# Reading the moving operands of the feed-forward products from the last column to the first

## The chip, the cores and the metric

The kernel runs on one core of a Trainium2 chip, as one launch. The metric is the device time of that launch in microseconds, on the slowest core, which here is the only one. A time is given as the median of several runs. All durations of single instructions come from one further execution that the hardware profiler recorded.

## What is computed

Windowed attention over 4 batches, 8 heads, 768 positions and 64 numbers per head, with block summaries as additional keys, and then a feed-forward layer over the 3072 tokens of 512 numbers (2048 hidden units). Cut to what matters:

```python
k_sum = k.reshape(B, H, nb, block, D).max(axis=3)      # block = 32, nb = 24
v_sum = v.reshape(B, H, nb, block, D).mean(axis=3)
scores = concat([where(|i - j| < 16, q k^T / 8, -1e9), q k_sum^T / 8 + log(block)])
x = softmax(scores) @ concat([v, v_sum])               # heads side by side: 3072 x 512
h = x @ w_in                                           # 512 -> 2048
g = s * maximum(h, 0)**2 + b
out = g @ w_out                                        # 2048 -> 512
```

Everything is float32, and the result is wanted close to float32.

## The kernel before

**Chunks.** The 3072 tokens are cut into 12 chunks `c` of T = 256 tokens, three to a batch. For each chunk the attention is done in four head pairs `p`, and then the feed-forward layer over 16 slices `f` of 128 hidden units.

**Attention.** `scores` (L280) makes the scores of 64 positions against a window of 96 keys and the 24 block keys. VectorE masks them (L323), ScalarE takes the exponentials (L336), VectorE normalizes (L346), and the weights are turned so that the keys stand on the partitions: for chunks 0 to 2 by TensorE (`transposes`, L379), later by VectorE (L368). `values` (L397) multiplies the turned weights `pT` with the values `vw`: the values are the stationary operand, 64 columns of `pT` the moving one, and the result `pav` in PSUM has 64 rows per head and 256 tokens in its columns. So each sub-block `i` of 64 tokens is written to its own 64 columns of `pav` (L413 to L417). For chunk 0 `values_of_means` (L388) adds the block summaries in matmuls of their own. `attended` and `attended_low` copy `pav` to SBUF as `x`.

**Split operands.** The two products of the feed-forward layer are done with operands in a rounded float32 form (`fp32r`). Each operand is held as a high part, rounded to that form, and a low part, the rest: `xh` and `xl` for x, `wh` and `wl` for the weights (both products' weights of a slice `f` in one tile of 1024 columns, 512 for the first and 512 for the second), `gh` and `gl` for g. A product is the sum of three matmuls: low by high, high by low, high by high.

**First product.** `hidden` (L454), for a chunk and a slice: 12 matmuls at L460, for the three terms and the four parts `kc` of 128 of the 512 inputs. The stationary operand is 128 columns of the weights, the moving operand is `x[:, kc]`, 128 partitions by 256 tokens. Two slices share a PSUM tile `ph`. For the first two slices of chunk 0 the same is done at L441 (`first_products`) as the parts of x come.

**Between.** ScalarE takes relu (L468) and square (L474), GpSimd scales and shifts (L481), and a copy and a subtraction make `gh` (L219 or L221) and `gl` (L492).

**Second product.** `project` (L495): 6 matmuls at L504 for a chunk and a slice, two halves `t` of 128 tokens by three terms. The stationary operand is 128 token columns of g, the moving operand is `w[:, 512:]`, the 512 output weights, accumulated over all 16 slices in two PSUM tiles `po`, which `evict` copies out and stores.

**Order.** The order of the work is written down: for the start of the program in a list (`FIRST_ORDER`), and after that by a plan of steps that places four slices of the first product (48 matmuls), then four of the second (24), and between them the attention of a later chunk. Each engine goes through its own queue in that order. All weights are loaded, scaled, converted and split once in the first 100 us or so and then stay in SBUF. `laid_out` arranges the inputs on the host; the weights travel as 64-bit words and are brought to float32 on the chip.

Of the kernel before, what the change touches and what calls it, by code (L numbers as in the profile page):

```python
# [19 lines left out]
P = 128  # L20
B, H, S, D = 4, 8, 768, 64
DM, DFF = 512, 2048
BLOCK = 32
WINDOW = 16
SUB = 64
WIN = SUB + 2 * WINDOW
NB = S // BLOCK
KR = WIN + NB
NSUB = 4
T = NSUB * SUB  # L30
# [5 lines left out]
NF = DFF // P  # L36
# [3 lines left out]
def win_start(st):  # L40
    return min(max(SUB * st - WINDOW, 0), S - WIN)
# [3 lines left out]
def windowed_attention_then_relu2_ffn(ctx, tc, qk, vwin, kt, vt, kq, vrow, wp, out):  # L45


    nc = tc.nc
# [98 lines left out]
    kraw, ksum, vraw, vhalf, vsum = {}, {}, {}, {}, {}  # L147
# [128 lines left out]
    def together(c):  # L276

        return c >= 2
# [109 lines left out]
    def values_of_means(p):  # L388
        pT, o = pT_of.pop((0, p)), o_of[0, p]
        for i in range(NSUB):  # L390
            for e in range(2):
                nc.tensor.matmul(
                    o[64 * e : 64 * e + 64, i * SUB : (i + 1) * SUB], vsum[0][0:KR, 2 * p + e],
                    pT[:KR, e * T + i * SUB : e * T + (i + 1) * SUB], start=False, stop=(i == NSUB - 1),
                )

    def values(c, p):  # L397
        vw, pT = vw_t.pop((c, p)), pT_of[c, p] if c == 0 else pT_of.pop((c, p))
        if c == 0 and p % 2:
            o_of[c, p] = ps_po.tile([P, DM], F32, name="pav", tag="po")  # L400
        elif c < 2 or p % 2 == 0:
            if c == 2:
                o_of[c, p] = ps_s.tile([P, 2 * T], F32, name="pav", tag="ps")
            elif together(c) and p:
                o_of[c, p] = ps_t.tile([P, 2 * T], F32, name="pav", tag="pt")
            else:
                o_of[c, p] = ps_v.tile([P, 2 * T], F32, name="pav")
            if c > 1:
                o_of[c, p + 1] = o_of[c, p][:, T:]
        o = o_of[c, p]  # L410
        for i in range(NSUB):
            for e in range(2):
                oi, pi = o[64 * e : 64 * e + 64, i * SUB : (i + 1) * SUB], pT[:, e * T + i * SUB : e * T + (i + 1) * SUB]  # L413
                if c == 0:
                    nc.tensor.matmul(oi, vw[0:WIN, e, i, :], pi[0:WIN], start=(i == 0), stop=False)
                else:
                    nc.tensor.matmul(oi, vw[:KR, e, i, :], pi[:KR], start=True, stop=True)  # L417
# [17 lines left out]

    ph_of, gg, po = {}, {}, {}

    def first_products(ph, w, x, low, kc, first, last):
        k = slice(kc * P, (kc + 1) * P)
        for n, (a, b) in enumerate(((w_l[w], x), (w_h[w], low), (w_h[w], x))):  # L440
            nc.tensor.matmul(ph, a[:, k], b[:, kc], start=(first and n == 0), stop=(last and n == 2))  # L441

    def hidden_pair(c, f):
        if f % 2 == 0:
            ph_of[c, f // 2] = ps_h.tile([P, 2 * T], F32, name="ph", tag="ph")
        return ph_of[c, f // 2][:, (f % 2) * T : (f % 2 + 1) * T]

    def hidden_part(f, kc):
        if kc == 0:
            hidden_pair(0, f)  # L450
        ph = ph_of[0, f // 2][:, (f % 2) * T : (f % 2 + 1) * T]
        first_products(ph, f, xt[0], xl[0], kc, kc == 0, kc == NKC - 1)

    def hidden(c, f):  # L454
        ph = hidden_pair(c, f)
        terms = [
            (w[f], x, kc) for w, x in ((w_l, xt[c]), (w_h, xl[c]), (w_h, xt[c])) for kc in range(NKC)
        ]
        for n, (w, x, kc) in enumerate(terms):
            nc.tensor.matmul(  # L460
                ph, w[:, kc * P : (kc + 1) * P], x[:, kc], start=(n == 0), stop=(n == len(terms) - 1)
            )

    def activate(c, q, other=0):
# [30 lines left out]
    def project(c, f):  # L495
        if f == 0:
            for t in range(T // P):
                pool, tag = ((ps_t, "pt"), (ps_v, "pav"))[t] if c == 1 else (ps_po, "po")
                po[c, t] = pool.tile([P, DM], F32, name="po", tag=tag)
        gh, gl = (g[:, (f % 2) * T : (f % 2 + 1) * T] for g in gg[c, f // 2])  # L500
        terms = [(gl, w_h[f]), (gh, w_l[f]), (gh, w_h[f])]
        for t in range(T // P):
            for n, (a, w) in enumerate(terms):
                nc.tensor.matmul(  # L504
                    po[c, t], a[:, t * P : (t + 1) * P], w[:, 512:],
                    start=(f == 0 and n == 0), stop=(f == NF - 1 and n == len(terms) - 1),
                )

# [38 lines left out]
    def of(fn, *more):  # L547
# [5 lines left out]
        "u": load_unit, "x": load_values, "L": load_k,  # L553
        "W": keep_warm, "K": k_max, "k": fill_k, "Z": scores_of_maxima, "S": scores, "M": masked, "E": exps,
        "N": normalize, "T": transposes, "C": turned, "V": values, "U": values_of_means, "R": mean_of_rows,
        "F": mean_done, "t": fill_v, "X": attended, "y": attended_low, 
        "Ai": of(scale_weights, "in"), "Ao": of(scale_weights, "out"), "A": of(scale_weights, "both"),
        "Bi": of(convert_weights, "in"), "Bo": of(convert_weights, "out"), "D": of(convert_weights, "both"),
        "Y": hidden_part, "H": hidden, "J": activate, "G": scaled, "a": upper_rows, "b": lower_rows,
        "P": project, "O": evict, "h": upper_weights, "l": lower_weights,  # L560
    }
    ahead = set()
# [19 lines left out]
    for c in range(2, NC):  # L582
        bi, ci = place(c)
        for p in range(NPAIR):
# [3 lines left out]
            m, e0, e1, n, fv, tr, tu, va, xa = (base + lag for lag in lags)  # L588
# [17 lines left out]
            if turns_on_dve(c):  # L606
                for u in range(8):
                    a, k = divmod(u + 8 * (p % 2), 4)
                    then(base + TURN_AT[2 * p + u // 4], TURN, turned_blocks, c, p // 2, a, k)
            else:  # L610
                then(tr, PE_ATT, transposes, c, p)
                then(tu, CHAIN, turned, c, p)
            then(va, VISIT, values, c, p)
            if p % 2 == 0:
                then(xa, ATT, attended, c, p)
# [4 lines left out]
    for i in range(NF, NC * NF):  # L620
        c, f = divmod(i, NF)

        then(i - i % 4, HID, hidden, c, f)
        if f % 2:
            for stage_of in (activate, scaled, upper_rows, lower_rows):
                then(i, CHAIN, stage_of, c, f // 2)
        then((i + 4) | 3, PROJ, project, c, f)
        if f == NF - 1:
            for t in range(T // P):
                then((i + 4) | 3, EVICT, evict, c, t)  # L630
# [7 lines left out]
def laid_out(q, k, v, moe_w_in, moe_w_out, moe_s, moe_b):  # L638

    import numpy as np  # L640

    def turn(x):
        return x.reshape(B, NPAIR, 2, S, D).transpose(0, 1, 2, 4, 3).reshape(B, NPAIR, P, S)

    qT, kT = turn(q), turn(k)
    kq = np.concatenate([kT[0], qT[0, :, :, :T]], axis=-1)
    qk = np.zeros((NC - 1, NPAIR, P, T + NSUB * KR + 2), np.float32)
    qk[..., -2:] = np.concatenate([moe_s, moe_b])
    vwin = np.zeros((NC, NPAIR, P, 2, NSUB, D), np.float32)
    for c in range(NC):  # L650
        bi, ci = divmod(c, PER_B)
        kw = np.zeros((NPAIR, P, NSUB, KR), np.float32)
        for i in range(NSUB):
            w = win_start(NSUB * ci + i)
            kw[:, :, i, :WIN] = kT[bi, :, :, w : w + WIN]
            vwin[c, :, :WIN, :, i] = v[bi, :, w : w + WIN].reshape(NPAIR, 2, WIN, D).transpose(0, 2, 1, 3)
        if c > 0:
            qk[c - 1, :, :, :-2] = np.concatenate(
                [qT[bi, :, :, ci * T : (ci + 1) * T], kw.reshape(NPAIR, P, NSUB * KR)], axis=-1
            )  # L660
    vt = v.reshape(B, 2, 4, NB, BLOCK, D).transpose(0, 1, 2, 3, 5, 4).reshape(B, 2, 4 * NB, D, BLOCK)
    vrow = v[0].transpose(1, 0, 2).reshape(3, 2, P, H * D).transpose(0, 2, 1, 3)
    w_in = moe_w_in.view(np.int64).reshape(NKC, P, NF, P).transpose(2, 1, 0, 3).reshape(NF, P, 512)
    w_out = moe_w_out.view(np.int64).reshape(NF, P, DM)
    return {"qk": qk, "vwin": vwin, "kt": kT, "vt": vt, "kq": kq, "vrow": vrow, "wp": np.stack([w_in, w_out], axis=1)}


# [23 lines left out]
```

## Time and profile before

| what | value |
|---|---|
| median of 3 runs | 615.12 us (614.93 to 615.46) |
| span of the profiled execution | 614.0 us |
| what lies around the span, against the median | 1.1 us |
| instructions in the span | 13522 |
| matmuls | 5240, of them 3456 in the rounded form (2304 of 256 columns at L460 and L441, 1152 of 512 at L504) |
| granted TensorE clock | 1.000 |
| moved by DMA | 66.41 MB, 108 GB/s on the mean |

The times of runs and the profiled execution are different executions, so the span is compared with the median only through the 1.1 us. A profile's mean duration of a matmul is that of its record, from its start to its result. Records of neighbours overlap. How fast matmuls follow each other is read from start to start, or from the length of a piece of the chain divided by its count.

### The profile page before, as it was taken

Reading aid. Unit: us, or ns where it says so; the run is one execution under the profiler, and the core shown is the slowest. Engines: PE = TensorE matmul, PEld = TensorE weight load, DVE = VectorE, ACT = ScalarE, POOL = GpSimd, SP = SyncE. Lnnn points to the kernel's source line nnn. Section 1 sums busy time; section 2 is a strip of 40 time slices with the busy share of each in tenths; the row PEclk is TensorE's granted clock in tenths of the full one; section 3 lists DMA queues with packets and bytes.
Section 4 is the critical chain, followed back from the end, with each engine's and each line's share of the span. In section 5 each row is a group of like instructions: output and inputs, shape, how many; then the busy total and the mean of one; then the engine's idle time right before and its main releaser. Section 6 shows DMA issues by size and latency. Waiting matters only on the chain.

```text
span 614.0 us, 13522 instructions
## 1 busy us (share of the span) xinstructions
PE 602.5 (98%) x5240; PEld 545.7 (89%) x5240; DVE 418.2 (68%) x1126; ACT 276.3 (45%) x712; POOL 138.8 (23%) x275
## 2 busy tenths in 40 slices
PE   6999999999999999999999999999999999999997
PEld 5788899899889998999999899999998999999896
DVE  6999998789489378668758648847848927832211
ACT  5989998262352262263163254235235236223221
POOL 4321012111411411412131411331141151141110
PEclk9999999999999999999999999999999999999999
DMA  8999723026205016103503112500710500200000
GB/s 336 388 394 366 268 83 112 4 96 177 85 3 184 1 45 233 47 20 104 170 20 113 73 45 61 220 18 20 220 55 1 185 4 16 86 1 1 36 1 35
DMA packets 26993, 66.41 MB, mean 108 GB/s; under 512 B 3824, under 2 KB 3824, under 8 KB 26928
## 3 DMA queue, kind: packets, MB, share of 16 engines
q1 hardware_dynamic: 26928, 65.54, 30.3%
q8 instruction: 41, 0.67, 0.4%
q14 instruction: 24, 0.20, 0.1%
HBM read 59.09 MB, written 6.29 MB: 106 GB/s over the span
## 4 chain that ended last, share of the span: by engine, by line
PE 88%; DVE 4%; ACT 3%; DMA 3%; issue 1%; SPq 1%; POOL 0%; POOLq 0%; ACTq 0%; DVEq 0%
PE po L504 40%; PE ph L460 39%; PE pav L417 3%; PE ps L301 3%; ACT pr L336 2%; DVE pT L368 2%; DMA wraw<-in_wp_dram 1%; DMA vsum<-vmean 1%; PE warm L199 1%; DVE pr L346 1%; DMA kq<-in_kq_dram 1%; PE pt L379 1%; SPq L180 0%; POOL vw L263 0%; DVE gl L492 0%
## 5 line engine op out<-in xcount | busy, mean ns | idle before, releaser
L481 POOL TENSOR_SCALAR r<-r,sb_col 128x512 f32<-128x512 f32 x85 | 69.6, 819 | 389.9 <-ACT r L474 247.0
L504 PE MATMUL po<-wh,gl 128*128 128x512 f32 x384 | 150.9, 393 | 0.0
L504 PE MATMUL po<-wl,gh 128*128 128x512 f32 x384 | 149.6, 390 | 0.0
L504 PE MATMUL po<-wh,gh 128*128 128x512 f32 x384 | 149.5, 389 | 0.0
L468 ACT ACTIVATE r<-ph 128x512 f32<-128x512 f32 x93 | 55.3, 595 | 204.9 <-PE ph L460 192.5
L219 DVE CAST gh<-r 128x512 fp32r<-128x512 f32 x88 | 37.7, 429 | 139.5 <-POOL r L481 135.9
L368 DVE STREAM_TRANSPOSE pT<-pr 32x256 f32<-32x256 f32 x288 | 125.5, 436 | 4.1
L460 PE MATMUL ph<-xh,wl 128*128 128x256 f32 x760 | 120.9, 281 | 0.6 <-ACT r L468 0.6
L460 PE MATMUL ph<-xl,wh 128*128 128x256 f32 x760 | 120.2, 281 | 0.0
L460 PE MATMUL ph<-xh,wh 128*128 128x256 f32 x760 | 120.2, 281 | 0.0
L460 PEld LDWEIGHTS ph<-xh,wl 128*128 128x128 f32 x760 | 106.2, 189 | 5.6 <-ACT r L468 1.2
L460 PEld LDWEIGHTS ph<-xh,wh 128*128 128x128 f32 x760 | 103.3, 190 | 0.0
L460 PEld LDWEIGHTS ph<-xl,wh 128*128 128x128 f32 x760 | 102.6, 189 | 0.0
L504 PEld LDWEIGHTS po<-wh,gh 128*128 128x128 f32 x384 | 72.0, 188 | 15.1
L504 PEld LDWEIGHTS po<-wh,gl 128*128 128x128 f32 x384 | 72.1, 188 | 14.5 <-issue 1.0
L504 PEld LDWEIGHTS po<-wl,gh 128*128 128x128 f32 x384 | 72.1, 188 | 12.8
L336 ACT ACTIVATE pr<-pr,mn 128x120 f32<-128x120 f32 x176 | 66.9, 382 | 22.8 <-DVE mn L323 22.7
L492 DVE TENSOR_TENSOR gl<-r,gh 128x512 fp32r<-128x512 f32 x96 | 69.2, 721 | 3.7 <-ACT gh L221 0.9
L474 ACT ACTIVATE r<-r 128x512 f32<-128x512 f32 x92 | 58.1, 632 | 5.3 <-DVE r L470 2.4
L263 POOL COPY vw<-vsum 24x256 f32<-24x256 f32 x88 | 46.8, 564 | 36.9 <-DMA vsum<-vmean 21.8
L346 DVE TENSOR_TENSOR pr<-pr,rs 128x480 f32<-128x480 f32 x48 | 32.5, 678 | 2.4 <-ACT pr L336 0.5
L221 ACT COPY o<-po 128x512 f32<-128x512 f32 x23 | 13.5, 587 | 45.2 <-PE po L504 44.2
(88 smaller groups left out, 479.3 us busy)
## 6 DMA issues: line engine op xcount, KB each, us to landing
wraw<-in_wp_dram SPq DMA_DIRECT2D x32, 512.0 KB
qk<-in_qk_dram SPq DMA_DIRECT2D x44, 369.0 KB
vw<-in_vwin_dram SPq DMA_DIRECT2D x48, 256.0 KB
out_dram<-o SPq DMA_DIRECT2D x24, 256.0 KB
kraw<-in_kt_dram SPq DMA_DIRECT2D x12, 384.0 KB
vraw<-in_vt_dram SPq DMA_DIRECT2D x12, 252.0 KB
kq<-in_kq_dram SPq DMA_DIRECT2D x4, 512.0 KB
vraw<-in_vt_dram SPq DMA_DIRECT2D x6, 264.0 KB
```

The source lines that it names most:

```text
L219: nc.vector.tensor_copy(out_, in_)
L263: nc.gpsimd.tensor_copy(vw_t[c, p][WIN:KR, e], vsum[bi][WIN : WIN + NB, 2 * p + e, :].unsqueeze(1).to_broadcast([NB, NSUB, D]),)
L301: nc.tensor.matmul(o, qi, kw[r, i, :], start=True, stop=True)
L336: nc.scalar.activation(pr, pr, AF.Exp, bias=mn_of[c, p][:, n : n + 1], scale=-1.0, accum_out=sm_of[c, p][:, n : n + 1])
L346: nc.vector.tensor_tensor(pr, pr, rs.unsqueeze(2).to_broadcast([P, 4, KR]), ALU.mult)
L368: nc.vector.transpose(to[BLOCK * k : BLOCK * (k + 1), :, rows], src)
L460: nc.tensor.matmul(ph, w[:, kc * P : (kc + 1) * P], x[:, kc], start=(n == 0), stop=(n == len(terms) - 1))
L468: nc.scalar.activation(r, ph, AF.Relu)
L474: nc.scalar.activation(r, r, AF.Square)
L481: (nc.vector if other else nc.gpsimd).tensor_scalar(g, g, s_col, b_col, ALU.mult, ALU.add)
L492: nc.vector.tensor_tensor(gl, g, gh.bitcast(F32), ALU.subtract)
L504: nc.tensor.matmul(po[c, t], a[:, t * P : (t + 1) * P], w[:, 512:], start=(f == 0 and n == 0), stop=(f == NF - 1 and n == len(terms) - 1),)
```

## The change

Of the matmuls of both products the moving operand is now given with its last column first: the access steps by -1 through the 256 columns of `x[:, kc]` and through the 512 columns of `w[:, 512:]`. So that the results come out in the same places, these operands lie in reversed order. The columns of `w_out` are reversed by the host in `laid_out`. The tokens of x are reversed by `values` and `values_of_means`: they write sub-block `i` to the 64 columns counted from the far end, and read their own moving operand, the 64 columns of `pT`, backwards. The stationary operands, the scores, the results in `ph` and `po`, and everything behind them are as they were.

```diff
@@ values_of_means
                 nc.tensor.matmul(
-                    o[64 * e : 64 * e + 64, i * SUB : (i + 1) * SUB], vsum[0][0:KR, 2 * p + e],
-                    pT[:KR, e * T + i * SUB : e * T + (i + 1) * SUB], start=False, stop=(i == NSUB - 1),
+                    o[64 * e : 64 * e + 64, T - (i + 1) * SUB : T - i * SUB], vsum[0][0:KR, 2 * p + e],
+                    backwards(pT[:KR, e * T + i * SUB : e * T + (i + 1) * SUB]), start=False, stop=(i == NSUB - 1),
                 )
@@ values
-                oi, pi = o[64 * e : 64 * e + 64, i * SUB : (i + 1) * SUB], pT[:, e * T + i * SUB : e * T + (i + 1) * SUB]
+                oi = o[64 * e : 64 * e + 64, T - (i + 1) * SUB : T - i * SUB]
+                pi = backwards(pT[:, e * T + i * SUB : e * T + (i + 1) * SUB])
@@
+    def backwards(moving):
+
+        return moving[:, ::-1]
+
     def first_products(ph, w, x, low, kc, first, last):
         k = slice(kc * P, (kc + 1) * P)
         for n, (a, b) in enumerate(((w_l[w], x), (w_h[w], low), (w_h[w], x))):
-            nc.tensor.matmul(ph, a[:, k], b[:, kc], start=(first and n == 0), stop=(last and n == 2))
+            nc.tensor.matmul(ph, a[:, k], backwards(b[:, kc]), start=(first and n == 0), stop=(last and n == 2))
@@ hidden
-                ph, w[:, kc * P : (kc + 1) * P], x[:, kc], start=(n == 0), stop=(n == len(terms) - 1)
+                ph, w[:, kc * P : (kc + 1) * P], backwards(x[:, kc]), start=(n == 0), stop=(n == len(terms) - 1)
@@ project
-                    po[c, t], a[:, t * P : (t + 1) * P], w[:, 512:],
+                    po[c, t], a[:, t * P : (t + 1) * P], backwards(w[:, 512:]),
@@ laid_out
-    w_out = moe_w_out.view(np.int64).reshape(NF, P, DM)
+    w_out = moe_w_out.view(np.int64).reshape(NF, P, DM)[..., ::-1]
```

The list of instructions of every engine, their order and their waits are the same before and after; only the line numbers of the kernel differ.

## The prediction

> **What bounds the kernel now.** I read the profile page first, its busy times and its chain of waits, because they say which engine a change has to touch to be seen.
>
> ```profile
> PE 602.5 (98%) x5240; PEld 545.7 (89%) x5240; DVE 418.2 (68%) x1126; ACT 276.3 (45%) x712; POOL 138.8 (23%) x275
> PEclk9999999999999999999999999999999999999999
> PE 88%; DVE 4%; ACT 3%; DMA 3%; issue 1%; SPq 1%; POOL 0%; POOLq 0%; ACTq 0%; DVEq 0%
> PE po L504 40%; PE ph L460 39%; PE pav L417 3%; PE ps L301 3%; ACT pr L336 2%; DVE pT L368 2%; DMA wraw<-in_wp_dram 1%; DMA vsum<-vmean 1%; PE warm L199 1%; DVE pr L346 1%; DMA kq<-in_kq_dram 1%; PE pt L379 1%; SPq L180 0%; POOL vw L263 0%; DVE gl L492 0%
> ```
>
> TensorE is 88% of the chain, and two lines are 79% of it: L504 (second product) and L460 (first product). The clock row shows full clock in every slice. A busy PE says nothing yet of its pace, and the span's mean mixes stages, so next comes the table of windows, then the chain in order of time inside the long even stretch.
>
> ```profile
> 0.00:30.00 30.00, 23.86 (x441) 19.33 (x441) 23.38 (x98) 23.20 (x86) 12.71 (x47) 1.00 0.95 363
> 30.00:60.00 30.00, 29.26 (x261) 26.19 (x262) 27.75 (x53) 27.80 (x39) 5.79 (x10) 1.00 1.00 394
> 60.00:100.00 40.00, 40.00 (x288) 36.04 (x287) 35.65 (x58) 39.64 (x81) 6.34 (x9) 1.00 0.50 180
> 169.42:600.00 430.58, 430.58 (x3556) 393.86 (x3556) 276.40 (x790) 156.67 (x437) 96.61 (x177) 1.00 0.21 71
> ```
>
> Columns after the stretch: length, then busy time of PE, weight loads (PEld), DVE, ACT and POOL, the granted clock, the DMA share, GB/s. From 169 to 600 us PE never pauses (430.58 of 430.58) and nobody else is near: DVE 276, ACT 157. In the first 60 us the DMA share is 0.95 to 1.00 and from 60 to 100 us ACT is busy 39.64 of 40, so there a faster matmul would wait for weights; I count no gain before 100 us.
>
> ```profile
> 175.09 5.65 PE ph L460 x48
> 180.74 5.44 PE po L504 x24
> 100.00:614.00 514.00, 241.74 (x1992) 240.66 (x1992) 1.00 0.22 71
> 100.00:614.00 514.00, 243.50 (x1034) 190.30 (x1032) 1.00 0.22 71
> ```
>
> The first two rows are pieces of the chain (start, length): 48 matmuls of L460, 256 columns each, take 5.65 us, 117.7 ns each; 24 of L504, 512 columns each, take 5.44 us, 226.7 ns each. The mean durations on the page, 281 and 390 ns, are longer because neighbours overlap; the pace is what counts. The last two rows are the windows of L460 and of L504 alone, from 100 us on: 1992 and 1034 matmuls, and in the second place their weight loads. So 1992 x 117.7 ns = 234.5 us and 1034 x 226.7 ns = 234.4 us: 469 of those 514 us are set by these two paces. Each nanosecond on every one of the 3026 is 3.0 us.
>
> **What the paces contain.** Is there anything to gain or lose in how a matmul reads? Two more places show other paces for TensorE.
>
> ```profile
> 52.43 0.62 PE L460 MATMUL ph<-xh,wh 128*128 128x256 f32 x4
> ...
> 56.97 0.39 PE L504 MATMUL po<-wh,gl 128*128 128x512 f32 x1
> 108.92 1.03 PE L379 MATMUL pt<-ident,pr 128*120 128x128 f32 x8
> L379 PE MATMUL pt<-ident,pr x48: 270/273/326, 12.7 to 109.7; 128*120 128x128 f32 x48
> ```
>
> From 52.43 to 56.97 us ten rows of four L460 matmuls stand one behind the other (the first is shown, and the matmul after the last): 40 in 4.54 us, 113.5 ns each. The same instruction, with the same weights, needs 117.7 ns later. L379 turns full float32 tiles: eight in 1.03 us of which the last one's own 273 ns record is the tail, so (1.03 - 0.273)/7 = 0.108, about 109 ns for 128 columns. That form has half the columns of L460 for nearly its time; I take it as two steps per column, 109/256 = 0.426 ns each. The rounded float32 matmuls read a fresh four-byte column on every step and pay 226.7/512 = 0.443 and 113.5/256 = 0.443 in their quick state, 117.7/256 = 0.460 in the usual one. So 0.017 ns of each column (8.7 ns of each L504), plus the 4.2 ns between the two states of L460, are time that the array's step does not explain. The forms that read fastest pay it, hence I take it for the moving read's.
>
> **The change part by part.** Nothing is moved: every engine has the same instructions in the same order with the same waits and the same DMAs. Three things change in them.
>
> (a) The moving operand of the 3456 rounded matmuls (2304 of 256 columns, 1152 of 512) starts at its last column and steps by -1. The trace of before has no operand that is walked down, so this price is bounded from both sides. Best: the read costs only the 0.426 of L379. L504 goes to 512 x 0.426 = 218.0 ns, saving 8.7 x 1034 = 9.0 us; L460 to 109.0 ns, saving 8.7 x 1992 = 17.3 us; together 26.3 us, and 8.7 x 3456 = 30.1 us if the first 100 us gained as well. Worst: the read falls to L379's time per column, 109/128 = 0.852 ns, worked out under the rivals.
>
> The value I take for L460 is not the best one. In its own window the weight loads are busy 240.66 of 241.74 us: one load follows the other without a gap, and the change leaves the loads alone. The shortest pace that a row shows with a load for each matmul is 113.5 ns, so L460 gets 4.2 ns, not 8.7: 4.2 x 1992 = 8.4 us. L504 has slack there (190.30 of 243.50), so its whole 8.7 counts: 9.0 us. Sum: 17.4 us.
>
> The Trainium skill, page "TensorE: Matmul & The Clock Gate", section "Back-to-back issue gap", gives N/2.4 + 2.5 ns per warm matmul, which is 215.8 and 109.2 ns here; the trace of before does not agree (226.7 and 117.7). If walking down reached that, an estimate by the page is 10.9 x 1034 + 8.5 x 1992 = 28 us saved, 587 us.
>
> (b) The attention values (L417 and the like) read the turned weights backwards and write their 64-column pieces from the far end, so that x lies reversed. L417 has 640 matmuls after 100 us.
>
> ```profile
> L417 PE MATMUL pav<-pT,vw 120*64 120x64 f32 x640 | 21.4, 224 | 1.1 <-POOL vw L263 1.1
> ```
>
> They are 21.4 us busy in all, full float32 with the slower step, which leaves the read slack as in L379: I cost them at nothing. Were the cover gone and each took twice as long, 21 us. Which piece is written first cannot matter, since the copies of x wait for the last.
>
> (c) The output weights come reversed from the host: the same bytes in the same DMAs, and the scaling, converting and splitting work element by element. Nothing.
>
> If L504 and L460 shorten by 17 us, what is late next? In the even stretch DVE is busy 276 of 430 us and ACT 157; losing 17 of 430 us takes DVE from 64% to 67%. No new bound.
>
> The profiled execution has a span of 614.0 us, the median of the runs is 615.12, so 1.1 us lies around the span. The sum: 614.0 - 17.4 + 1.1 = 597.7 us.
>
> **The rivals.** *No change.* The read costs what it costs in either direction: a column is a column, and the lost 0.017 ns per column is the rate of this data form, not of its order. For it: L504's pace is twice L460's quick one almost exactly (226.7 against 2 x 113.5 = 227.0), the mark of a rate, and a rate has no reason to ask for a direction. Against it: the 113.5 and 117.7 for one instruction, so the rate is not fixed. It gives 614.0 + 1.1 = 615.1 us. The Trainium skill, page "SBUF — State Buffer", section "Specifications (TRN2)", says that SBUF has 16-byte lines and that two hits on a line are enough for full bandwidth; four neighbouring float32 columns share a line whichever end comes first, so by that rule nothing changes here; no run shows it for a step of -1 yet.
>
> *Half of the gain.* Only one of the two parts comes: L460 settles in its quick state and L504 stays (615.1 - 8.4 = 606.7), or L504 gains and L460 stays bound by its loads (615.1 - 9.0 = 606.1). I count it with the forecast, as its upper end.
>
> *Slower.* A read that runs ahead of the array upwards may not do so downwards. Then every moving column of L460 and L504 costs a step of its own, at worst L379's 0.852 ns: L504 436 ns (+209), L460 218 ns (+100), that is 1034 x 0.209 + 1992 x 0.100 = 216 + 199 = 415 us, 1030 us in all. For it: these forms pay more per column than any other, so they have no slack to hide a slower read. Against it: nothing in the kernel walks down, so nothing shows such a cost. It decides early: 0.41 ns more per matmul makes 1.23 us over 3026, which is 0.2% of 615 and about what a measurement of this kernel can tell from no change. A mild form, 4.2 ns for each as between the two states of L460, would be 12.7 us, 628 us.
>
> *The change does nothing in the instruction* (the step is put back in order on its way) is the first rival again, with the same time.
>
> **How the numbers follow.** Faster has 0.46: the missing time is there, it varies for one and the same instruction, and the moving read is the only thing the change touches. No change has 0.34, because the double pace of L504 speaks for a rate. Slower has 0.20. The likeliest case gives 597.7, rounded to 598; its own range is 584 (30.1 us saved, and a little) to 607 (half of the gain). The range given reaches from there over no change, to 617, a little above 615.5, the highest run of before; only slower, with 0.20, is left out.
>
> **What would show it.** Right: in the chain after, 24 of L504 take about 5.23 us instead of 5.44 and 48 of L460 about 5.45 instead of 5.65, with the weight loads of L460 still without a gap; the same counts and order; DVE and ACT as busy as before in microseconds. The first rival: 5.44 and 5.65 again. The slower one: pieces of 24 beyond 5.5 us, and L460 longer in the same measure per column. The forecast is wrong if L504 does not move at all, or if L460 goes below 113 ns, since then the loads did not bind it; if L417's 640 leave 21 us by more than 2 us, part (b) was not free.

## The result, and the profile after

The changed kernel takes 621.75 us (median of 4 runs, 621.60 to 622.56) against 615.18 us (4 runs, 614.93 to 615.46): slower, by a ratio of 1.0109, 95% interval 1.0095 to 1.0123. The profiled execution has a span of 620.0 us against 614.0 us, so the profile shows 6.0 of the 6.6 us.

The engines' busy times after, from the page, show where the time can be:

```profile
PE 610.1 (98%) x5240; PEld 547.0 (88%) x5240; DVE 419.0 (68%) x1126; ACT 277.0 (45%) x712; POOL 137.6 (22%) x275
```

TensorE is busier by more than 1 us, 610.1 us against 602.5, with the same 5240 matmuls; no other engine is. The lines of its code have moved: L465 is the first product (L460 before), L509 the second (L504 before), L418 the values (L417 before). The chain of waits after, in order of time, in the same part of the program as the two pieces of before:

```profile
175.39 5.65 PE ph L465 x48
181.04 5.60 PE po L509 x24
```

The reader compares 5.65 with 5.65 and 5.60 with 5.44. Four slices of the first product take as long as before. Four slices of the second product take 0.16 us longer, 5.60/24 = 233.3 ns for a matmul instead of 226.7. Then the windows of both lines from 100 us to the end, and the group of the values in that stretch:

```profile
100.00:620.00 520.00, 242.10 (x1992) 240.91 (x1992) 1.00 0.21 70
100.00:620.00 520.00, 250.12 (x1034) 190.62 (x1032) 1.00 0.21 70
L418 PE MATMUL pav<-pT,vw 120*64 120x64 f32 x640 | 21.2, 224 | 0.4 <-POOL vw L263 0.4
```

L465 is busy 242.10 us (241.74 before), L509 250.12 us (243.50 before), L418 21.2 us (21.4 before). The loss is in the second product: 6.6 us more for its busy time, and 1034 x 6.7 ns = 6.9 us by the paces. Not all of it reaches the end. The first even run of 24 starts at 169.59 us after and at 169.42 us before, so only 0.17 us is lost up to there; behind that point stand 912 matmuls of the second product, and 912 x 6.7 ns = 6.1 us, close to the 6.0 us by which the two spans differ.

### The profile page after: what moved, and what is told of

Same layout as the page of the kernel before. It is cut to its first block, busy times and chain, and to the rows that moved or that the text cites. A ratio compares the mean times of both kernels' runs of the same rounds, so it can differ in the third digit from the quotient of the medians.

```text
span 620.0 us, 13522 instructions
## 1 busy us (share of the span) xinstructions
PE 610.1 (98%) x5240; PEld 547.0 (88%) x5240; DVE 419.0 (68%) x1126; ACT 277.0 (45%) x712; POOL 137.6 (22%) x275
## 4 chain that ended last, share of the span: by engine, by line
PE 88%; DVE 5%; ACT 3%; DMA 1%; issue 1%; POOL 0%; SPq 0%; POOLq 0%; DVEq 0%
PE po L509 41%; PE ph L465 40%; PE pav L418 3%; PE ps L301 3%; ACT pr L336 2%; DVE pT L368 2%; DVE pr L346 1%; DMA kq<-in_kq_dram 1%; PE pt L379 1%; DVE vhalf L172 1%; DMA vsum<-vmean 0%; POOL vw L263 0%; DVE gl L497 0%; PE ph L446 0%; DVE pr L323 0%
## 5 line engine op out<-in xcount | busy, mean ns | idle before, releaser
L509 PE MATMUL po<-wh,gl 128*128 128x512 f32 x384 | 153.9, 401 | 0.0
L509 PE MATMUL po<-wl,gh 128*128 128x512 f32 x384 | 152.6, 397 | 0.0
L509 PE MATMUL po<-wh,gh 128*128 128x512 f32 x384 | 152.6, 397 | 0.0
L465 PE MATMUL ph<-xh,wl 128*128 128x256 f32 x760 | 120.9, 282 | 0.0
L465 PE MATMUL ph<-xh,wh 128*128 128x256 f32 x760 | 120.7, 281 | 0.0
L465 PE MATMUL ph<-xl,wh 128*128 128x256 f32 x760 | 120.2, 281 | 0.0
L465 PEld LDWEIGHTS ph<-xh,wl 128*128 128x128 f32 x760 | 106.5, 188 | 5.1 <-DVE wl L144 0.2
L465 PEld LDWEIGHTS ph<-xl,wh 128*128 128x128 f32 x760 | 102.8, 188 | 0.0
L465 PEld LDWEIGHTS ph<-xh,wh 128*128 128x128 f32 x760 | 102.8, 188 | 0.0
L509 PEld LDWEIGHTS po<-wh,gh 128*128 128x128 f32 x384 | 72.2, 188 | 17.4
L509 PEld LDWEIGHTS po<-wh,gl 128*128 128x128 f32 x384 | 72.2, 188 | 16.3 <-issue 1.1
L509 PEld LDWEIGHTS po<-wl,gh 128*128 128x128 f32 x384 | 72.2, 188 | 14.7
L221 ACT COPY o<-po 128x512 f32<-128x512 f32 x23 | 13.5, 587 | 47.2 <-PE po L509 45.9
```

Of the source, the lines that this page charges most:

```text
L465: nc.tensor.matmul(ph, w[:, kc * P : (kc + 1) * P], backwards(x[:, kc]), start=(n == 0), stop=(n == len(terms) - 1))
L509: nc.tensor.matmul(po[c, t], a[:, t * P : (t + 1) * P], backwards(w[:, 512:]), start=(f == 0 and n == 0), stop=(f == NF - 1 and n == len(t ...
```

## The experiments

Fifteen further kernels were run: e1 to e8 are variants of the whole kernel, p1 to p7 are the kernel before with series of further matmuls behind its last product. The theory that the two traces suggest: a moving operand of 512 columns that is read downwards costs 6.7 ns more, for a reason to be found, and the first product hides it. The first rival: the reversed x or the values carry part of the loss. Further rivals came from what the runs showed.

### Which of the two products

One kernel reverses only the output weights, another only x.

```diff
 e1_second_only, against the changed kernel
-        ... backwards(b[:, kc]) ... backwards(x[:, kc])      # and values, values_of_means
+        ... b[:, kc] ... x[:, kc]                            # x lies forward again
```

> Only the output weights are reversed and read backwards (L504); x and the attention values stay forward. Two theories agree here, a cost per column and a fixed cost per matmul of the downward read: the whole loss sits in the second product, 1034 x 6.7 ns after 100 us, so 621 to 622 us against 615.2 and 24 of these matmuls in 5.60 us. The rival, that the reversed x or the values carry part of it, gives 617 to 620.

Measured: 622.15 us, ratio 1.0107 (1.0094 to 1.0121).

```diff
 e2_first_only, against the changed kernel
-                    po[c, t], a[:, t * P : (t + 1) * P], backwards(w[:, 512:]),
+                    po[c, t], a[:, t * P : (t + 1) * P], w[:, 512:],
...                                                          # and w_out lies forward again
```

> Only x is reversed: the values write it from the far end and the first product reads it backwards; the output weights stay forward. If the first product is held by its back-to-back weight loads (117.7 ns), 615.2 us within 0.2%, with 48 of its matmuls in 5.65 us. If the reversed x carries part of the loss, 617 to 619.

Measured: 616.07 us, ratio 1.0011 (1.0002 to 1.0020): some 0.1%, and by its interval hardly nothing. Pieces of its chain:

```profile
175.84 5.65 PE ph L465 x48
181.49 5.44 PE po L509 x24
```

The first product reads downwards here and takes the same 5.65 us. So the loss of the change is that of the second product, and reversing x and the values is free to within 0.2%.

### Size, and what a matmul costs by itself

For p1 and the other runs named p, the kernel before got series of 24 matmuls behind its last product. They are extra work and write to a spare PSUM tile; their moving operand is the high weights of slices 0 and 1, their stationary operand the last `gh`. One line of code for each series:

```diff
+        for k in range(24): nc.tensor.matmul(big, gh[:, k % 4 * P : k % 4 * P + P], w[:, 512:1024], start=True, stop=True)
+        for k in range(24): nc.tensor.matmul(big, gh[:, k % 4 * P : k % 4 * P + P], w[:, 512:1024][:, ::-1], start=True, stop=True)
```

> The kernel before, with 17 series of 24 further matmuls behind the last product that write to a spare PSUM tile: 512, 384 and 256 columns with 128 weight columns, 512, 256 and 128 with 32 weight columns, each forward and backward; then 512 columns from 1 and from 8 columns further on, each way. A cost per column: backward minus forward 6.7, 5.0, 3.3, 1.7 ns for 512, 384, 256, 128 where the weights are short. A fixed cost per matmul: 6.7 ns at every size with short weights. If it comes from the weight load beside it, the short weights take most of it away (under 3 ns at 512). If it hangs on where the read starts in memory, the shifted series differ from the others by some ns.

The timeline of this kernel behind its last product, one row for a series: start, length of the 24, line, operands, weight shape, moving shape. The last matmul's own record (0.22 to 0.40 us) is the tail of a length, and the next series starts before it; a pace is therefore the difference of two starts, divided by 24.

```profile
609.63 5.60 PE L522 MATMUL probe<-wh,gh 128*128 128x512 f32 x24
615.07 5.77 PE L523 MATMUL probe<-wh,gh 128*128 128x512 f32 x24
620.68 4.36 PE L524 MATMUL probe<-wh,gh 128*128 128x384 f32 x24
624.87 4.42 PE L525 MATMUL probe<-wh,gh 128*128 128x384 f32 x24
629.13 3.04 PE L526 MATMUL probe<-wh,gh 128*128 128x256 f32 x24
...
634.86 5.72 PE L528 MATMUL probe<-wh,gh 128*32 128x512 f32 x24
640.42 5.76 PE L529 MATMUL probe<-wh,gh 128*32 128x512 f32 x24
646.02 2.90 PE L530 MATMUL probe<-wh,gh 128*32 128x256 f32 x24
648.76 2.99 PE L531 MATMUL probe<-wh,gh 128*32 128x256 f32 x24
651.59 1.60 PE L532 MATMUL probe<-wh,gh 128*32 128x128 f32 x24
653.03 1.61 PE L533 MATMUL probe<-wh,gh 128*32 128x128 f32 x24
...
665.86 5.76 PE L536 MATMUL probe<-wh,gh 128*128 128x512 f32 x24
```

512 columns forward (L522): (615.07 - 609.63)/24 = 226.7 ns, backward (L523): 5.61/24 = 233.8. These are the two paces of the kernels, so the series measure the thing itself. With 32 weight columns the 256 columns of L530 and L531 need 2.74 and 2.83 us, 114.2 and 117.9 ns, and 128 columns 60.0 both ways (1.44 us each). The cost is no fixed amount for each matmul: with 32 weight columns it is nothing at 128 columns and nearly 4 ns at 256; with 128 weight columns it is 3 ns at 384 (174.6 and 177.5) and 7 ns at 512. The length of the weights matters too. With 32 weight columns the 512 columns of L528 and L529 differ by only 1.7 ns, 231.7 and 233.3, but that is because the forward read has become slower, not the backward one quicker. The surprise is L536: forward, but from 8 columns further on. It takes as long as a backward read. From 1 column further on both ways are slower still, 238.8 forward and 235.8 backward. So the direction is not the whole matter.

The next series, p2, takes the columns in other orders.

> The kernel before, with 12 series of 24 matmuls of 512 columns behind the last product: forward; backward; groups of 4 columns forward with the columns in each backward; groups of 4 backward with the columns in each forward; the same two with groups of 16; groups of 4 all forward; every second column forward and backward; every fourth column forward and backward; forward again. If the cost is in the order inside a group of 4, the third series is slow (233) and the fourth quick (227). If it is in going from a group to the one before it, the other way round. If the cost is per column whatever the pattern, every series with a step down lies at 233 or more. If a step away from 1 is what costs, every second column costs as much forward as backward.

```profile
609.98 5.60 PE L522 MATMUL probe<-wh,gh 128*128 128x512 f32 x24
615.42 5.77 PE L523 MATMUL probe<-wh,gh 128*128 128x512 f32 x24
621.02 5.63 PE L524 MATMUL probe<-wh,gh 128*128 128x512 f32 x24
626.48 5.77 PE L525 MATMUL probe<-wh,gh 128*128 128x512 f32 x24
632.09 6.56 PE L526 MATMUL probe<-wh,gh 128*128 128x512 f32 x24
...
649.56 11.03 PE L529 MATMUL probe<-wh,gh 128*128 128x512 f32 x24
660.41 11.38 PE L530 MATMUL probe<-wh,gh 128*128 128x512 f32 x24
671.61 11.25 PE L531 MATMUL probe<-wh,gh 128*128 128x512 f32 x24
```

In the order of the expectation: forward 5.60; backward 5.77; groups of four rising with the columns in each backward (L524) 5.63, quick; groups of four falling with the columns in each forward (L525) 5.77, slow; groups of sixteen rising with the columns in each backward (L526) 6.56, the slowest of all (6.39/24 = 266 ns). So the step of -1 is not what costs. Inside a group of four the order is free; the order of the groups is not. Every second column (L529 forward, L530 backward) needs twice the time, 452 and 467 ns; every fourth (L531) hardly more, 461 (the row behind it starts at 682.68).

### The same inside the kernel

```diff
 e3_fours, against e1_second_only
-        return moving[:, ::-1]
+        return moving.rearrange("p (n k) -> p n k", k=4)[:, :, ::-1]
-    w_out = moe_w_out.view(np.int64).reshape(NF, P, DM)[..., ::-1]
+    w_out = moe_w_out.view(np.int64).reshape(NF, P, DM // 4, 4)[..., ::-1].reshape(NF, P, DM)
```

> Only the output weights change: they lie, and are read, with the columns inside every group of four reversed, while the groups come in rising order. If the order of groups is what costs, as the series suggest (226.7 ns), 615.2 us within 0.2%. If a step of -1 costs by itself, 621 to 622 us.

Measured: 615.63 us, ratio 1.0003 (0.9994 to 1.0012). All 512 columns are read with a step of -1 inside their fours, and nothing is lost.

The opposite, e5, `[:, ::-1, :]` with the weights laid out to match, lets the groups fall and the columns in them rise.

> Only the output weights change: groups of four columns come last group first, the columns in each group forward. If going down from group to group costs, or a start that is not at a multiple of 16 columns (this one starts at column 1020 of the tile), 621 to 622 us; if the step of -1 is what costs, 615.2 us.

Measured: 622.74 us, ratio 1.0115 (1.0097 to 1.0133). The falling groups carry the whole loss.

```diff
 e4_shifted, against the kernel before
-                    po[c, t], a[:, t * P : (t + 1) * P], w[:, 512:],
+                    po[c, t], a[:, t * P : (t + 1) * P], w[:, 504:1016],
```

> Nothing is reversed: the second product reads forward, but 8 columns earlier (columns 504 to 1015 of the weight tile instead of 512 to 1023), so the output is that of other weights. If the loss hangs on the start within 16 columns, as the shifted series suggests (233 ns), 621 to 622 us without any step down. If only the direction costs, 615.2 us.

Measured: 621.26 us, ratio 1.0101 (1.0084 to 1.0117). Without any step downwards, a start 8 columns earlier costs as much as the change.

### Where a read starts

> The kernel before, with 14 series of 24 matmuls of 512 columns and 128 weight columns behind the last product: forward from the first column of the half, then from 4, 12, 16, 32, 64 and 128 columns further on; backward from 4 and from 16 columns further on; blocks of 64, 128 and 256 columns taken last block first with the columns in each forward; groups of 8 columns forward with the columns in each backward; forward again. Theory A, the loss is paid at each step down from one group of four columns to another or one block to another: blocks of 64, 128, 256 have 7, 3 and 1 such steps and lie near 227 ns. Theory B, the loss hangs on where in a block of 16 columns the read starts or ends: forward from 4 and 12 on costs 233 like the shift by 8 did, from 16, 32, 64 and 128 on 227, and the big blocks, which start at such a place, 227 as well. Theory C, any start other than the first column of the half costs it: all shifts and all block orders 233.

In p3, shifts of 4, 12, 16, 32, 64 and 128 columns (L523 to L528, all forward; that of 12 is left out below), and blocks of 64 columns in falling order (L531):

```profile
614.00 5.72 PE L523 MATMUL probe<-wh,gh 128*128 128x512 f32 x24
...
625.15 5.76 PE L525 MATMUL probe<-wh,gh 128*128 128x512 f32 x24
630.75 5.74 PE L526 MATMUL probe<-wh,gh 128*128 128x512 f32 x24
636.33 5.65 PE L527 MATMUL probe<-wh,gh 128*128 128x512 f32 x24
641.82 5.60 PE L528 MATMUL probe<-wh,gh 128*128 128x512 f32 x24
...
658.47 5.60 PE L531 MATMUL probe<-wh,gh 128*128 128x512 f32 x24
```

The shifts up to 32 columns are slow (231 to 233 ns), that of 64 is nearly back (5.49/24 = 228.8, and its later matmuls follow each other at 227), that of 128 is back at 5.60. Falling blocks of 64 columns (and of 128 and 256, 5.60 as well) are as quick as a plain forward read. Of the three theories A is nearest for the blocks and none holds for the shifts: the unit is 64 columns, not 16. What happens from one block of 64 to the next is free; what costs is the start of the read within 64 columns, or the order of the groups in it.

### Relative to what

The next question was whether the place counts by itself or relative to the stationary operand, whose load goes on beside the read.

> The kernel before, with 14 series of 24 matmuls of 512 columns behind the last product, in which the place of the stationary operand within its tile is varied too: forward with the 128 weight columns from 0, 16, 32 and 64 columns on; moving and stationary both 32 and both 16 further on; backward with the weights 16 and 32 further on; backward with both 16 further on; moving 32 and weights 16 further on; forward with 32 weight columns from 32 on, with 64 from 0 and from 32 on; forward again. Theory R, the weight load and the moving read disturb each other and only their places relative to each other count: weights 16 or 32 further on make the forward read slow (231 to 234), 64 on does not (227), and some of the pairs in which both are shifted are quick again. Theory M, the moving read alone loses time when it does not walk whole blocks of 64 columns upwards: the place of the weights changes nothing, 227 forward and 233 backward throughout, and 233 where the moving operand is shifted.

In p4, forward with the weights 0, 16, 32 and 64 columns further on (L522 to L525), then moving and stationary operand both 32 (L526) and both 16 further on (L527), then backward with the weights 16 further on (L528):

```profile
610.02 5.60 PE L522 MATMUL probe<-wh,gh 128*128 128x512 f32 x24
615.46 5.76 PE L523 MATMUL probe<-wh,gh 128*128 128x512 f32 x24
621.06 5.74 PE L524 MATMUL probe<-wh,gh 128*128 128x512 f32 x24
626.63 5.61 PE L525 MATMUL probe<-wh,gh 128*128 128x512 f32 x24
632.08 5.61 PE L526 MATMUL probe<-wh,gh 128*128 128x512 f32 x24
637.52 5.62 PE L527 MATMUL probe<-wh,gh 128*128 128x512 f32 x24
642.97 5.76 PE L528 MATMUL probe<-wh,gh 128*128 128x512 f32 x24
```

This decides it for the forward read. The moving operand of L523 and L524 lies where it always did; only the weights have moved, and the pace goes to 233 and 232 ns. With both shifted alike (L526, L527) it is back at 227. Theory M falls, and what theory R asked for came: with 128 weight columns the forward read is quick where the two places are equal modulo 64 columns. Away from there the relative place does not give the pace by itself: a moving operand 32 on with weights 16 on gave 229.6 ns, and weights alone 48 on (p6) 229.2, with the same distance of 16 modulo 64 as the moving operand alone 16 on, 233.3. Nor are equal places enough for shorter weights: with 32 and 64 weight columns from the first column on, the forward read took 231.7 ns (L528 of p1) and 230.0 (p4). So it may be the moments at which load and read pass the same place that count, and not the places alone; that is not shown. All places are counted from the start of a tile; where the tiles themselves start in memory, no view shows.

Two kernels put it into the second product.

```diff
 e6_weights_shifted, against the kernel before
-        gh, gl = (g[:, (f % 2) * T : (f % 2 + 1) * T] for g in gg[c, f // 2])
+        gh, gl = gg[c, f // 2]
...
+                at_col = ((f % 2) * T + t * P) % 384 + 16
-                    po[c, t], a[:, t * P : (t + 1) * P], w[:, 512:],
+                    po[c, t], a[:, at_col : at_col + P], w[:, 512:],
 e7_both_shifted: the same, and
+                    po[c, t], a[:, at_col : at_col + P], w[:, 464:976],
```

> Nothing is reversed and the moving operand lies as before; the second product takes its 128 weight columns 16 columns further on in the tiles of g (the last block wraps to the first), so the output is that of shifted tokens. Theory R: the second product slows as with the backward read, 233 ns, 621 to 622 us. Theory M: 615.2 us within 0.2%.

Measured: 618.06 us, ratio 1.0047 (1.0031 to 1.0062): less than theory R gave. Its chain shows why:

```profile
174.86 5.46 PE ph L460 x48
180.32 5.59 PE po L505 x24
185.91 5.66 PE ph L460 x48
```

The second product (L505) is slow at 5.59 us as theory R has it. But every other run of 48 of the first product takes 5.46 us instead of 5.65, though nothing was changed in it: it gives back part of the loss.

> Nothing is reversed. The second product takes its weight columns 16 further on, as in the run before with shifted weights, and its moving operand 48 columns earlier (columns 464 to 975), which is 16 further on modulo 64; the output is that of other operands. If the relative place modulo 64 columns decides, the second product is quick again, 24 in 5.44 us, and the time is 615.2 us or a little less. If every shift costs by itself, 621 us or more.

Measured: 615.17 us, ratio 1.0002 (0.9993 to 1.0011), with 24 of the second product in 5.44 us again:

```profile
179.89 5.44 PE po L505 x24
185.33 5.65 PE ph L460 x48
```

Two shifts, each of which costs, cost nothing together.

### Is a backward read only a forward read at a bad place?

> The kernel before, with 15 series of 24 matmuls of 512 columns and 128 weight columns behind the last product: forward; backward with the weights 4, 8, 24, 40, 48, 56 and 63 columns further on; blocks of 64, 32 and 128 columns taken in rising order with the columns in each backward; forward with the weights 4, 8 and 48 further on; forward again. Theory R1, only the relative place counts and the backward read is a forward read at a bad place: at one or more of the seven places the backward read is quick (227). Theory R2, a read that goes down inside the 64 columns is slow at every place: all seven at 231 to 236, and the blocks of 64 and 128 with the columns backward as well.

In p6, two of the seven backward series, and the blocks of 64 columns in rising order with the columns in each backward (L530):

```profile
614.75 5.76 PE L523 MATMUL probe<-wh,gh 128*128 128x512 f32 x24
...
648.36 5.76 PE L529 MATMUL probe<-wh,gh 128*128 128x512 f32 x24
653.96 5.76 PE L530 MATMUL probe<-wh,gh 128*128 128x512 f32 x24
```

The answer is no. With the weights 4, 8, 24, 40, 48, 56 and 63 columns further on (and 0, 16 and 32 in the earlier series) a backward read takes 233 to 234 ns, without exception. Going down inside the 64 columns is slow at every place that was tried. Theory R2 holds.

### Why the first product loses next to nothing

> The same with 15 series of 256 columns, as the first product has: forward with the weights 0, 8, 16, 32, 48 and 64 columns further on; backward with 0 and 32; both 16 further on; backward with 16; moving 32 on with weights 0 and 32; 64 weight columns forward and backward; forward again. Theory R: the pace changes with the weights' place, between 113 and 120 ns. Theory M: 113 to 118 forward wherever the weights lie, 117.8 backward.

In p5, forward with 128 weight columns, then forward and backward with 64 (L534, L535), 256 columns each:

```profile
611.52 3.03 PE L522 MATMUL probe<-wh,gh 128*128 128x256 f32 x24
...
645.83 2.89 PE L534 MATMUL probe<-wh,gh 128*64 128x256 f32 x24
648.55 2.99 PE L535 MATMUL probe<-wh,gh 128*64 128x256 f32 x24
651.38 3.02 PE L536 MATMUL probe<-wh,gh 128*128 128x256 f32 x24
```

With 128 weight columns all series lie between 118 and 120 ns, forward and backward and wherever the operands lie: neither theory's price shows. With 64 weight columns the forward read takes 2.72/24 = 113.3 ns and the backward one 2.83/24 = 117.9. So there is a cost of some 4 ns at 256 columns, and in these series something else, which comes with the longer weight load, holds the pace at or above that already.

But that something is not constant: 113.4 and 117.7 ns both occur in the kernel before, for the same instruction. And the change does bear on which one comes. The first row is the stretch of the kernel before from which the prediction took its 113.5 ns, the second the same stretch of the changed kernel:

```profile
51.58 5.55 PE ph L460 x48
50.91 5.67 PE ph L465 x48
```

Near 125 us the same 48 matmuls take 5.46 us in e1, which reads x upwards, and 5.66 us in e2, which reads it downwards. From start to start, every one of the fifteen kernels that read x upwards has stretches of the first product at 113.3 ns, in the kernel before 6 of the 56 runs of 12 or more. In the two that read it downwards, the changed kernel and e2, not one of the 56 runs has such a stretch; all settle at about 117.8. This fits p5: read downwards, 256 columns did not settle below 117 ns anywhere. It is nearly unseen in the time because the kernel before keeps to 117.7 in almost all of its runs already, and has the quick ones before 131 us, where little of what TensorE loses reaches the end. Two runs, p7 and e8, tried to find what else chooses.

> The kernel before, with 18 stretches behind the last product: 12 matmuls of 512 columns, then none, one or two other matmuls (64, 128, 192, 384, 448 columns; 256 with the weights 16 or 32 further on, the moving operand 32 further on, fewer weight columns or backward; 512 with the weights shifted), then 24 matmuls of 256 columns as in the first product. If the first product's two paces are two states that the start of a run of matmuls chooses, some stretches lie at 113.4 ns and others at 117.8 to 120, with nothing changed in the 24 themselves. If the pace belongs to the places of the operands, all 18 are alike.

Measured: all 18 stretches settle at about 120 ns. No separator brought the quick pace, so the state could not be set in that way.

```diff
 e8_scores_later, against the kernel before
-                then(base, VISIT, scores, c, p, j)
+                then(base, PROJ + 0.5, scores, c, p, j)
```

> Nothing is reversed; only the scores of the next chunk move behind the four slices of the second product, so that in each chunk one run of 48 of the first product follows the scores and not the second product. If the pace of the first product is a state that the start of its run chooses, and a start behind something else gives the quick one, 9 runs of 48 save 4.4 ns each, 1.9 us: 613.3 us. If the state does not follow from what ran before, 615.2 us.

Measured: 634.42 us, ratio 1.0315 (1.0289 to 1.0341), which neither side expected. A piece of its chain and a row of TensorE's waits (us in total, times, the longest):

```profile
174.34 1.25 ACT pr L336 x6
...
175.67 5.71 PE ph L460 x48
```

```profile
PE ph L460 <- ACT pr L336: 13.5, 8, 1.7
```

The scores now come just ahead of the first product, whose PSUM tiles wait for the masking and the exponentials of the scores (TensorE waits 13.5 us in the eight longest places). On the question itself the run is undecided: of the runs of 48 behind the same predecessor, those that start at 175.7 and 276.2 us settled at 113.3 ns from start to start and those at 225.8 and 328.5 us at 117.8. The kind of predecessor alone does not choose.

## Why the prediction was wrong

**What bounds the kernel: right.** TensorE's pace in two lines sets the time. No other line of TensorE moved by as much as 0.5 us, and L509, busy 6.6 us longer, became 6.6 us of the run. That the two agree so exactly is in part chance: the spans of the two profiled executions differ by 6.0.

**What the paces contain: wrong, the failing step.** The prediction took 0.017 ns of each column "for the moving read's" time and let the change remove it: "L504 goes to 512 x 0.426 = 218.0 ns". Nothing in the trace linked that remainder to the direction, and 0.426 was borrowed from a float32 form of another kind. The measured 233.3 ns lies on the other side. In the series with 512 columns no pace below 226.6 ns settled: the kernel before already read in the best of the ways tried. The term that was to save 9.0 us cost 6.9.

**The 4.2 ns of the first product: wrong.** The prediction let the change bring the 113.5 ns of the early rows to all of the first product. The runs show the opposite: in both kernels that read x downwards that pace does not come up at all, and no run of 48 takes less than 5.65 us. The term of 8.4 us came out as nothing, because the long stretch from 169 us on stood at 117.7 before the change as well. The evidence for the weight loads was misread too:

```profile
L460 PEld LDWEIGHTS ph<-xh,wl 128*128 128x128 f32 x760 | 106.2, 189 | 5.6 <-ACT r L468 1.2
```

The record of one load is 189 ns long, more than the 117.7 ns from one matmul to the next, so the records overlap, and "one load follows the other without a gap" says nothing of a bound. That the load has a part in it is shown by the series: with 64 weight columns instead of 128 the forward read of p5 goes from 120 to 113.3 ns.

**Parts (b) and (c): right.** L418 is 21.2 us against 21.4, and x reversed alone changes the time by some 0.1%.

**The rivals.** The outcome is the slower one, of which 621.75 us lies halfway from no change (615.1) to its mild form (4.2 ns on each matmul, 628): it is 6.7 ns on the 1034 of the second product and nothing on the others. Its direction was right, a read downwards does not go as well as one upwards; that a read runs ahead of the array, as it had it, no run shows. And the cost is not in each step downwards. It is in falling order of the groups of four within 64 columns, whatever the order in the fours. The range ended at 617 and left this rival out, though it had a chance of 0.20.

The rule of the Trainium skill, page "SBUF — State Buffer", section "Specifications (TRN2)", that two hits on a 16-byte line are enough for full bandwidth, would have left the time unchanged. Inside the fours it agrees: their order is free (e3, 615.63 us). It does not tell of the falling groups (233.8 ns with four hits on each line), and with every second column, two hits on each line, the pace was 452 ns and not 227.

**Left open.** What in the chip makes 64 columns (256 bytes) the unit, whether the weight load and the moving read meet in the same part of the memory, and what, beside the direction, chooses between the two paces of the first product. The dependence on the weights' place shows that the two reads act on each other; that they collide in the memory was not shown. A read without a weight load beside it was not tried.

## What to carry to other kernels

With operands in the rounded float32 form and 128 weight columns, read the moving operand upwards, and let it and its weights start at the same place of their tiles modulo 64 columns: the two ways of missing that cost 3% of each matmul of 512 columns here, and two equal shifts cancel. An unexplained remainder in a pace is not a gain in waiting; a series of 24 matmuls behind the last product measures a disputed form for itself before a kernel is built on it. A cost can show in only one of two products that were changed alike, because the other is held by something else already; then look also at the places where the other was quick before.

## What the runs showed of the hardware that was not expected

- A stationary operand shifted by 16 columns slows the matmul of 512 columns from 226.7 to 233 ns with the moving operand unchanged; shifted by 64, it does not.
- Groups of sixteen in rising order with the columns in each backward take 266 ns, more than a read that is backward throughout (233.8).
- Every second column takes 452 ns and every fourth 461: leaving out columns doubles the time at once, and then hardly adds to it.
- With 32 weight columns instead of 128 a forward read of 512 columns is slower, 5.56/24 = 232 ns in the first series of sizes (its rows start at 634.86 and 640.42 us), not quicker.
- The same 48 matmuls of 256 columns take 5.46 or 5.65 us in the same kernel: nearly always 5.65 in the kernel before, in turn in e6, and never 5.46 where x is read downwards.
